# A cross network on one core: product 4 at a second level in both tiles, block 21's residual by DMA, weight loads reordered and held

## The chip, the core and the metric

The kernel runs on one core of a Trainium2 chip. The metric is the device time of one execution in microseconds (us), lower is better. The engines are called by the profile's names: PE is TensorE's matmul row and PEld its weight loads, DVE is VectorE, ACT is ScalarE, POOL is GpSimd, SP is SyncE, which here only issues DMAs.

## The reference

```python
B, F, D, L = 16384, 100, 16, 6
Din = min(F * D, 1024)              # 1024
# x0 [16384, 1024], ws [6, 1024, 1024], bs [6, 1024], all bfloat16
x = x0
for l in range(L):
    proj = jnp.einsum('bd,de->be', x, ws[l]) + bs[l]
    x = x0 * proj + x
return x
```

Six layers; in each, every row of `x` goes through a 1024 x 1024 matrix, gets a bias, is multiplied element by element with the first input, and is added to itself.

## The kernel before

**Tiles and units.** The 16384 rows are cut into 16 tiles of 1024 rows (`pr`, 0 to 15). Two tiles make a group (`grp`); in a group the tile with `lane` 0 and the one with `lane` 1 take turns, layer by layer. One tile in one layer is a unit; there are 96, in the order of `units`. A tile's state `x` lies transposed in one of three SBUF tiles `xst`, its first input in one of three `x0T`. So at any time one `xst` belongs to neither tile of the group: before layer 1 it still holds the output of the group before (its transposes out are issued in layer 0 of the second tile), and from layer 0 of the next group it holds that group's first tile.

**Seven products.** A unit's 1024 x 1024 x 1024 product is done by Strassen's scheme in the Winograd form: seven products of half size, P1 to P7, in place of eight. `T1` to `T4` are input combinations (VectorE), weights 5, 6, 7, 3 are weight combinations, made once in the first group and kept in DRAM (`Lc`). A product at one level is four groups (`m`) of four matmuls of 512 columns (`group`, line 318); its result is evicted from PSUM by ScalarE with the bias (`biased`, line 337). A product at the second level is again cut by seven: `inner` (line 506) issues seven groups of four matmuls of 256 columns, named `5p1` to `5p7` for product 5, and so on. It needs input sums of its own in `ti` tiles (`5t13`, `5t2`, `5t4`; products 2 and 3 share `23t2`, `23t4`), weights of its own (`5i`, `2i`, `3i`, `4i`), seven plain evictions or copies in place of four with bias (`copy`, line 327: two of the seven copy a partial sum from one PSUM bank into another, in which the next group goes on adding), and one more vector add (`5cc`).

Tile 0 and the last unit use one level only (`plain`). All other units have products 5, 2 and 3 at the second level (order list `PE_TWO`). Product 4 is there as well (`PE_FOUR`) where the lane is in `K4[l]`: both tiles in layer 0, the second tile alone in layers 1 to 4, none in layer 5.

**After the products.** The results lie in SBUF blocks `Q`, `U`, `V`, `W` (output blocks 11, 12, 22, 21), `P1s`, `P5s`, `C3`. VectorE adds them up (`Q1`, `Ua`, `Ub`, `Va`, and `Wa` where product 4 is at the second level), multiplies by the first input (`Qm`, `Um`, `Vm`, `Wm`) and adds to the state (`Qx` and so on). Blocks named in `DMA_RES[l]` do without that last vector instruction: GpSimd issues a DMA that adds the block into `xst` (line 563). Before, these are Q, U and V in layers 1 to 4. The names of the seven blocks turn from unit to unit by `NEXT`, so that a block still being read isn't written at once.

**Weights.** `wp` is a ring of 12 slots for 11 weights a layer (10 in layer 5). `ring_seq` is the order of the loads; `pump`, called after every step of the program, issues the next load on SP (line 247) as soon as the program order has passed the last use of the weight 12 places earlier. Both tiles use a loaded weight.

**Order.** Each step is an `Op` with the resources that it reads and writes, an engine and an estimated cost (`occ`, `lat`). `schedule` builds the dependencies, keeps TensorE's steps in the order of the lists at the top (`PE_FIRST` ... `PE_LAST`), and orders the other engines by due times reckoned back from TensorE; `ACCUM` is the latency it assumes for an accumulating DMA. The steps are then issued in that order, which is fixed on every engine. `fence` steps on POOL keep accumulations behind the output's transposes.

Of the kernel before, what the change touches and what calls it, by code (L numbers as in the profile page):

```python
# [9 lines left out]
ADD = mybir.AluOpType.add  # L10
# [12 lines left out]
P3.0 P4.3 P4.1 P4.0 P4.2  # L23
""".split()
PE_TWO = """
5p5 P1.1 5p1 P1.0 P1.3 5p2 2p5 5p6 2p1 P1.2 5p3 2p2 5p7 2p6 P6.0 5p4 2p3 3p5 2p7 3p1 P6.1 2p4 3p2 3p6 P6.2 P6.3 3p3
3p7 P7.0 P7.1 P7.2 3p4 P7.3 P4.1 P4.0 P4.3 P4.2
""".split()
PE_FOUR = """
5p5 P1.0 5p1 2p5 2p1 P1.1 5p2 5p6 2p2 P1.2 2p6 P1.3 5p3 5p7 2p3 2p7 P6.0 3p5 5p4 2p4 P6.1 P6.3 3p1 4p5 P6.2 4p1 3p2  # L30
P7.0 4p2 3p6 4p6 P7.1 3p3 4p3 4p7 P7.2 3p7 4p4 P7.3 3p4
""".split()
PE_LAST = """
P1.0 P1.1 P1.2 P1.3 P2.0 P2.1 P2.2 P2.3 P5.0 P5.1 P5.2 P5.3 P6.0 P6.1 P6.2 P6.3 P3.0 P3.1 P3.2 P3.3 P7.0 P7.1 P7.2 P7.3
# [2 lines left out]
ARRIVE = {"rows0": 4.9, "w0.1": 6.4, "rows1": 8.9, "rows2": 11.3, "w0.2": 11.9, "h0": 14.3, "h1": 15.5, "q": 17.5, "next": 21.0, "raw1": 40.0}  # L37


ACCUM = 9.0  # L40


class Op:
# [81 lines left out]
    return order, start, late  # L125


@with_exitstack
def kernel(
    ctx: ExitStack,  # L130
# [18 lines left out]
    KQ, HQ, NQ = KH // 2, H // 2, NB // 2  # L149
    RING = 12  # L150
    NDUMMY = 8
    K4 = {0: (0, 1), 1: (1,), 2: (1,), 3: (1,), 4: (1,)}
    DMA_RES = {1: "QUV", 2: "QUV", 3: "QUV", 4: "QUV"}

    const = ctx.enter_context(tc.tile_pool(name="const", bufs=1))
    dram = ctx.enter_context(tc.tile_pool(name="dram", bufs=1, space=bass.MemoryType.DRAM))
# [9 lines left out]
    xsts = [work.tile([P, 2, 2, KH, KH, P], BF16, name=f"xst{i}") for i in range(3)]  # L166
# [6 lines left out]
    ip["4"] = ip["2"]  # L173
    P1s, P5s, Q, U, V, W, C3 = (work.tile([P, KH, KH, P], BF16, name=f"ev{i}") for i in range(7))
    EV = {"5c": P5s, "3c": C3, "U": U, "V": V, "W": W, "Q": Q, "P1s": P1s}
    NEXT = {"5c": "3c", "3c": "5c", "U": "W", "V": "U", "W": "V", "Q": "Q", "P1s": "P1s"}
    home = {r: r for r in EV}
    TURNED, rows = ((0, 0), (1, 0), (0, 1)), (P1s, U, V)
    zeros = tin["4"][:, 0]
    ident = const.tile([P, P], BF16, name="ident")  # L180
# [35 lines left out]
    gl_of = lambda u: units[u][0] // 2 * L + units[u][1]  # L216
# [3 lines left out]
    ring_seq = []  # L220
    for gl in range(NGROUP * L):
        if gl < L:
            ring_seq += [(gl, w, "load") for w in RAW] + [(gl, w, "make") for w in MADE]
        else:
            ring_seq += [(gl, w, "load") for w in "1 5 5i 2 2i 6 3 3i 7 4 4i".split()[:11 if gl % L in K4 else 10]]
    slot = {(gl, w): f"slot{i % RING}" for i, (gl, w, _) in enumerate(ring_seq)}
    wt, uses_left, live = {}, {}, []
    pos = {"next": 0}
# [7 lines left out]
        live.append(key)  # L236
        return wt[key]

    def pump():
        while pos["next"] < len(ring_seq):  # L240
            gl, w, kind = ring_seq[pos["next"]]
            if kind == "make":
                return
            t = ring_tile((gl, w))
            if t is None:
                return
            nc.sync.dma_start(t[:], w_src(gl % L, w))
            pos["next"] += 1

    def ring_make(gl, w):  # L250
# [11 lines left out]
    ops, named = [], {}  # L262
# [6 lines left out]
    def op(name, eng, occ, lat, fn, rd=(), wr=(), weights=(), key=None, after=(), due=FAR, at=0.0):  # L269
        rd, wr = [at_home(r) for r in rd], [at_home(r) for r in wr]  # L270
        rd = tuple(rd) + tuple(slot[k] for k in weights if k in slot)
        for k in weights:
            uses_left[k] = uses_left.get(k, 0) + 1
        named[name] = len(ops)
        ops.append(Op(name, eng, occ, lat, fn, rd, tuple(wr), tuple(weights), key, tuple(named[a] for a in after), due, at))

    QD = ((0, 0), (0, 1), (1, 0), (1, 1))
    for u, (pr, l) in enumerate(units):
        one, first, last = plain(u), u == 0, u == NU - 1
        if not first:  # L280
            home = {r: home[NEXT[r]] for r in home}
        P1s, P5s, Q, U, V, W, C3 = (EV[home[r]] for r in ("P1s", "5c", "Q", "U", "V", "W", "3c"))
        CB = {"5": P5s, "2": Q, "3": C3, "4": W}
        gl, grp, lane = gl_of(u), pr // 2, pr % 2
        x0T, xst = x0Ts[pr % 3], xsts[pr % 3]
        xs = x0T if l == 0 else xst
        X0 = {q: f"x0.{pr % 3}.{q[0]}{q[1]}" for q in QD}
# [3 lines left out]
        kmajor = l == 0  # L291
# [15 lines left out]
        def ttop(name, o, a, b, o_, rd, wr, n=KH * NB, **kw):  # L307
            dve(name, lambda: tt(o, a, b, o_), n, rd, wr, **kw)
# [4 lines left out]
        def group(name, w, bank, bname, rhs, rname, m, start, gl=gl, kmajor=kmajor):  # L313
            def fn():
                for k in range(KH):
                    r = rhs[:, k, :] if kmajor else rhs[:, :, k, :]
                    o = bank[:] if kmajor else bank[:].rearrange("p (j r) -> p j r", r=P)
                    nc.tensor.matmul(o, lhsT=wt[(gl, w)][:, k, m * P:(m + 1) * P], rhs=r,  # L318
                                     start=(start and k == 0), stop=(k == KH - 1), skip_group_check=True)
# [30 lines left out]
        def fence(q, sp, u=u):  # L350
            def fn():
                nc.gpsimd.dma_start(seen[:], x0Ts[sp][0:1, q[1], q[0] * KH, 0:32])
            op(f"fence@{u}", "POOL", 0.6, 0.6, fn, [f"x0.{sp}.{q[0]}{q[1]}"], ["xbar"])

        if l == 0 and lane == 1:
            for q in QD:
# [119 lines left out]
        if not one:  # L476
            for X, a, b in (("5", 0, 1), ("2", 2, 3), ("3", 0, 1), ("4", 2, 3))[:len(inn)]:
# [12 lines left out]
                def inner(i, bank, start, X=X, gl=gl, q=q, tk=tk, src=src, kmajor=kmajor):  # L490
                    quad = {1: (0, 0), 2: (1, 0), 3: (1, 1)}
                    rhs = (lambda k: q(*quad[i], k)) if i in quad else (lambda k: tk({4: 3, 5: 0, 6: 2, 7: 1}[i], k))
                    rn = {1: src, 2: src, 3: src, 4: X + "t4", 5: X + "t13", 6: X + "t2", 7: X + "t13"}[i]
                    w = X if i in (1, 2, 4) else X + "i"

                    def fn():
                        if i in (1, 2, 4):
                            k0, e0 = {1: (0, 0), 2: (KQ, 0), 4: (KQ, HQ)}[i]
                            wv = wt[(gl, w)][:, k0:k0 + KQ, e0:e0 + HQ]
                        else:  # L500
                            wi = weight(gl, w) if gl < L else weight(gl, w)[:]
                            wv = wi.rearrange("p q (k e) -> p q k e", k=KQ)[:, {5: 0, 6: 1, 3: 2, 7: 3}[i]]
                        for m in range(KQ):
                            for k in range(KQ):
                                o = pX[bank][:, m * NQ:(m + 1) * NQ]
                                nc.tensor.matmul(o if kmajor else o.rearrange("p (j r) -> p j r", r=P), lhsT=wv[:, k, m * P:(m + 1) * P],  # L506
                                                 rhs=rhs(k), start=(start and m == 0 and k == 0), stop=(k == KQ - 1), skip_group_check=True)
# [38 lines left out]
        allm = lambda s: [f"{s}.{m}" for m in range(KH)]  # L546
        if not last:
            if not one:
                ttop("Q1", Q[:], Q[:], P1s[:], ADD, allm("Q") + allm("P1s"), allm("Q"))
            ttop("Ua", U[:], U[:], P5s[:], ADD, allm("U") + allm("5c"), allm("U"))  # L550
            if not one:
                ttop("Ub", U[:], U[:], C3[:], ADD, allm("U") + allm("3c"), allm("U"))
            if "4" in inn:
                ttop("Wa", W[:], W[:], V[:], ADD, allm("W") + allm("V"), allm("W"))
            ttop("Va", V[:], V[:], P5s[:], ADD, allm("V") + allm("5c"), allm("V"))
            for nm, C, q in (("Q", Q, (0, 0)), ("U", U, (0, 1)), ("V", V, (1, 1)), ("W", W, (1, 0))):
                if l == 0:
# [114 lines left out]
                op(f"sto{q[0]}{q[1]}.{pt}@{u}", "SP", 0.5, 8.0, sto, [sname], ())  # L672

    order, start, _ = schedule(ops)

    ctx.enter_context(tc.manual_schedule(
        engines={nc.tensor.engine, nc.scalar.engine, nc.vector.engine, nc.sync.engine, nc.gpsimd.engine}))
# [28 lines left out]
        load_half("4", h)  # L706
    nc.sync.dma_start_transpose(out=blk(x0Ts[0], 1, 1), in_=x0[NB:2 * NB, H:2 * H])

    held = [i for i in order if ops[i].name.startswith("ld") and ops[i].name.endswith(".1@1")]
    for i in held:  # L710
        ops[i].fn()
    for i in order:
        if i not in held:
# [4 lines left out]
        pump()  # L718


# [28 lines left out]
```

## Time and profile before

| | before |
|---|---|
| median of 3 runs | 2219.56 us (2219.45 to 2220.05) |
| the profiled execution | 2219.68 us, of which its span is 2217.9 us |
| busy: PE, DVE, ACT, POOL | 2208.2, 2144.3, 2037.4, 204.9 us |
| matmuls | 14625 |
| accumulating DMAs (line 563) | 192 of 512 KB |
| weight loads (line 247) | 475 of 512 KB |
| DMA share of two queues | 53.8% (issued by SP), 28.2% (issued by POOL) |
| granted TensorE clock | 0.999 |

The span reaches from the first to the last instruction; 1.8 us of the execution lie around it. Busy time is the union of an engine's instructions; matmuls overlap in the record, so that a matmul of 512 columns is shown with 379 ns although the next one starts 216 ns after it. Instructions of VectorE and ScalarE overlap by some 0.08 to 0.12 us in the same way. The DMA share is the part of the span in which the 16 DMA engines move packets of that queue.

### The profile page before, as it was taken

How to read it: one execution, taken by the hardware profiler on the slowest of the kernel's cores; microseconds unless marked ns; L12 is line 12 of the kernel's file. 1: busy time of each engine (PE TensorE's matmuls, PEld its weight loads, DVE VectorE, ACT ScalarE, POOL GpSimd, SP SyncE). 2: the span in 40 equal slices, each digit the busy share in tenths (PEclk: the TensorE clock that was granted, in tenths of full speed). 3: DMA queues.
4: the chain of work that ended last, by engine and by line, in shares of the span. 5: the costliest groups of instructions: out<-in, count | busy, mean ns of one | idle time of the engine just before them, and what ended most of it. 6: DMA issues, size and time to landing. Idle time of an engine off the chain costs nothing.

```text
span 2217.9 us, 39582 instructions
## 1 busy us (share of the span) xinstructions
PE 2208.2 (100%) x14625; PEld 1427.9 (64%) x14625; DVE 2144.3 (97%) x2527; ACT 2037.4 (92%) x3642; POOL 204.9 (9%) x263
## 2 busy tenths in 40 slices
PE   9999999999999999999999999999999999999998
PEld 5555566666666666666666666666666666666664
DVE  8999999999999999999999999999999999999997
ACT  7888899999999999999999999999999999999997
POOL 1122100110001100011000110011100111001110
PEclk9999999999999999999999999999999999999999
DMA  8777899768996689866898679986799877997777
GB/s 256 207 203 208 201 226 258 190 172 209 259 257 179 173 227 252 256 176 177 228 254 244 171 193 233 265 214 177 207 225 256 217 180 224 224 251 196 200 224 166
DMA packets 454306, 478.66 MB, mean 216 GB/s; under 512 B 269024, under 2 KB 381152, under 8 KB 454112
## 3 DMA queue, kind: packets, MB, share of 16 engines
q1 hardware_dynamic: 418352, 349.49, 53.8%
q0 software_dynamic: 35168, 126.38, 28.2%
q8 instruction: 114, 1.87, 0.3%
q14 instruction: 80, 0.66, 0.1%
q10 hardware_dynamic: 592, 0.27, 0.0%
HBM read 252.72 MB, written 58.20 MB: 140 GB/s over the span
## 4 chain that ended last, share of the span: by engine, by line
PE 98%; DMA 0%; DVE 0%; SPq 0%; issue 0%; POOLq 0%; ACT 0%; DVEq 0%; ACTq 0%
PE pA L318 52%; PE pX L506 43%; PE pX L318 3%; DMA wp<-in_ws_dram 0%; SPq L690 0%; DVE ev L204 0%; DMA xst<-x0T 0%; SPq L697 0%; DVE x0T L204 0%; DVE T L204 0%; POOLq L744 0%; ACT ev L337 0%; DVE x0T L421 0%; SPq L703 0%; SPq L700 0%
## 5 line engine op out<-in xcount | busy, mean ns | idle before, releaser
L506 PEld LDWEIGHTS <-wp 128*128 128x128 bf16 x8424 | 824.2, 98 | 272.3 <-issue 1.0
L337 ACT ACTIVATE ev<-pA,b_all 128x512 bf16<-128x512 f32 x1291 | 883.2, 691 | 114.2 <-PE pA L318 73.7
L318 PE MATMUL pA<-T,wp 128*128 128x512 bf16 x3856 | 924.0, 379 | 0.0
L318 PEld LDWEIGHTS <-wp 128*128 128x128 bf16 x5728 | 560.2, 98 | 493.8 <-issue 2.5
L327 ACT CAST ev<-pX 128x512 bf16<-128x512 f32 x1284 | 700.5, 596 | 22.5 <-PE pX L506 15.0
L506 PE MATMUL pX<-ti,wp 128*128 128x256 bf16 x4748 | 658.0, 273 | 0.0
L204 DVE TENSOR_TENSOR ev<-ev,ev 128x2048 bf16<-128x2048 bf16 x419 | 501.5, 1213 | 44.4 <-ACT ev L327 36.9
L204 DVE TENSOR_TENSOR ev<-ev,x0T 128x2048 bf16<-128x2048 bf16 (+1 forms) x324 | 383.9, 1204 | 1.0
L327 ACT COPY pX<-pX 128x512 f32<-128x512 f32 x628 | 364.6, 593 | 3.6
L318 PE MATMUL pA<-xst,wp 128*128 128x512 bf16 x1280 | 319.5, 379 | 0.0
L563 POOL DMA_DIRECT2D xst<-ev x192 | 166.0, 866 | 1294.6 <-ACT ev L337 491.9
L506 PE MATMUL pX<-xst,wp 128*128 128x256 bf16 x1736 | 260.4, 273 | 0.0
L506 PE MATMUL pX<-T,wp 128*128 128x256 bf16 x1588 | 238.2, 273 | 0.0
L204 DVE TENSOR_TENSOR ev<-ev,ip 128x1024 bf16<-128x1024 bf16 x314 | 209.2, 683 | 0.0
L204 DVE TENSOR_TENSOR T<-xst,T 128x2048 bf16<-128x2048 bf16 x160 | 194.8, 1217 | 2.5 <-PE pX L506 1.6
L204 DVE TENSOR_TENSOR T<-xst 128x2048 bf16<-128x2048 bf16 x160 | 194.8, 1217 | 0.1
L327 ACT CAST ip<-pX 128x512 bf16<-128x512 f32 x314 | 184.8, 589 | 0.4 <-PE pX L506 0.4
L204 DVE TENSOR_TENSOR xst<-ev,xst 128x2048 bf16<-128x2048 bf16 x124 | 150.7, 1217 | 0.0
L204 DVE TENSOR_TENSOR ti<-T,ti 128x512 bf16<-128x512 bf16 x272 | 113.4, 417 | 0.1
L204 DVE TENSOR_TENSOR ti<-xst 128x1024 bf16<-128x1024 bf16 x148 | 101.4, 685 | 8.3 <-PE pX L506 7.8
L204 DVE TENSOR_TENSOR ti<-xst,ti 128x1024 bf16<-128x1024 bf16 x148 | 101.2, 684 | 0.1
L204 DVE TENSOR_TENSOR ti<-T 128x1024 bf16<-128x1024 bf16 x136 | 92.9, 683 | 0.0
(57 smaller groups left out, 698.9 us busy)
## 6 DMA issues: line engine op xcount, KB each, us to landing
wp<-Lc SPq DMA_DIRECT2D x329, 512.0 KB, 6.1
xst<-ev POOLq DMA_DIRECT2D x192, 512.0 KB, 5.1
wp<-in_ws_dram SPq DMA_DIRECT2D x148, 512.0 KB, 6.8
out_dram<-x0T SPq DMA_DIRECT2D x60, 512.0 KB, 4.3
Lc<-wp POOLq DMA_DIRECT2D x24, 512.0 KB, 6.0
Lc<-xst POOLq DMA_DIRECT2D x23, 512.0 KB, 5.3
ev<-in_x_dram SPq DMA_DIRECT2D x3, 512.0 KB, 6.2
wp<-in_ws_dram SPq DMA_DIRECT2D x4, 256.0 KB, 7.5
```

What stands on the lines that cost most here:

```text
L204: nc.vector.tensor_tensor(out=o, in0=a, in1=b, op=op)
L318: nc.tensor.matmul(o, lhsT=wt[(gl, w)][:, k, m * P:(m + 1) * P], rhs=r, start=(start and k == 0), stop=(k == KH - 1), skip_group_check=True)
L327: act(name, lambda: nc.scalar.copy(out=dst, in_=src), rd, wr)
L337: act(name, lambda: nc.scalar.activation(out=dst, in_=src, func=IDENT, bias=b_all[:, c:c + 1], scale=1.0), rd, wr, True)
L506: nc.tensor.matmul(o if kmajor else o.rearrange("p (j r) -> p j r", r=P), lhsT=wv[:, k, m * P:(m + 1) * P], rhs=rhs(k), start=(start and m ...
L563: nc.gpsimd.dma_start(xblk(xst, *q), C[:], accum_op=ADD)
```

## The change

- **Product 4.** `K4` holds both tiles in layers 0 to 4: the first tiles of groups 1 to 7 do product 4 at the second level in layers 1 to 4 too. Layer 5 stays as it was.
- **Block 21.** `DMA_RES` names W as well in layers 1 to 4, so that `Wx` is an accumulating DMA and no vector instruction. `ACCUM` is 9.5.
- **Idle state tile.** In layers 1 to 4 of groups 1 to 7 the second tile's Q, U, V, W lie in the `xst` that belongs to neither tile. `lend` steps stand for the handover in the planner; they issue nothing. `NEXT` is another turn for the blocks that are left.
- **Orders.** `PE_TWO` and `PE_FOUR` hold the same groups in another order; `Ua` is listed after `Ub` and `Wa`.
- **Weight loads.** `LOAD_ORDER` is another order of the same loads. `plan_loads` gives each load from the second group on a planned time: as soon as its slot is free, but moved behind a planned accumulation that it would meet, and no later than `LEAD` + `LOAD` before its first use. `pump(time)` issues a load only when the program order has reached that time, and makes it wait for the newest matmul issued by then.

```diff
 PE_TWO = """
-5p5 P1.1 5p1 P1.0 P1.3 5p2 2p5 5p6 2p1 P1.2 5p3 2p2 5p7 2p6 P6.0 5p4 2p3 3p5 2p7 3p1 P6.1 2p4 3p2 3p6 P6.2 P6.3 3p3
-3p7 P7.0 P7.1 P7.2 3p4 P7.3 P4.1 P4.0 P4.3 P4.2
+5p1 2p5 5p5 P1.1 P1.0 5p6 2p1 5p2 P1.2 P1.3 5p3 2p2 5p7 2p6 P6.0 3p5 5p4 2p7 2p3 P6.1 3p1 P6.2 2p4 3p6 3p2 P7.0 P7.1
+P6.3 3p3 P7.2 3p7 P7.3 P4.0 P4.1 P4.3 3p4 P4.2
 PE_FOUR = """
-5p5 P1.0 5p1 2p5 2p1 P1.1 5p2 5p6 2p2 P1.2 2p6 P1.3 5p3 5p7 2p3 2p7 P6.0 3p5 5p4 2p4 P6.1 P6.3 3p1 4p5 P6.2 4p1 3p2
-P7.0 4p2 3p6 4p6 P7.1 3p3 4p3 4p7 P7.2 3p7 4p4 P7.3 3p4
+P1.1 5p5 5p1 2p5 P1.3 P1.0 5p2 2p1 5p6 P1.2 2p2 2p6 5p3 5p7 P6.0 2p3 3p5 2p7 P6.3 5p4 2p4 P6.2 3p1 P6.1 4p5 3p2 4p1
+3p6 P7.0 4p2 4p6 3p3 P7.1 4p3 3p7 4p7 P7.2 3p4 4p4 P7.3
...
-ACCUM = 9.0
+ACCUM = 9.5
+LOAD, BURST, LEAD = 1.45, 2.9, 8.0
+LOAD_ORDER = "1 5i 2i 5 2 6 3i 3 4i 4 7".split()
...
+def plan_loads(loads, bursts):
+    latest, nxt = [0.0] * len(loads), 1e9
+    for n in range(len(loads) - 1, -1, -1):
+        nxt = min(loads[n][1] - LEAD, nxt) - LOAD
+        latest[n] = nxt
+    busy, t = [], 0.0
+    for b in sorted(bursts):
+        t = max(t, b + 1.0)
+        busy.append((t, t + BURST))
+        t += BURST
+    issue, t = [], 0.0
+    for n, (free, _) in enumerate(loads):
+        s = max(free, t)
+        limit = max(s, latest[n])
+        for a, b in busy:
+            if b > s and a < s + 0.7 * LOAD:
+                s = b
+        t = min(s, limit)
+        issue.append(t)
+        t += LOAD
+    return issue
...
-    K4 = {0: (0, 1), 1: (1,), 2: (1,), 3: (1,), 4: (1,)}
-    DMA_RES = {1: "QUV", 2: "QUV", 3: "QUV", 4: "QUV"}
+    K4 = {l: (0, 1) for l in range(L - 1)}
+    DMA_RES = {l: "QUVW" for l in range(1, L - 1)}
...
-    NEXT = {"5c": "3c", "3c": "5c", "U": "W", "V": "U", "W": "V", "Q": "Q", "P1s": "P1s"}
+    NEXT = {"5c": "3c", "3c": "Q", "U": "U", "V": "W", "W": "V", "Q": "5c", "P1s": "P1s"}
...
-            ring_seq += [(gl, w, "load") for w in "1 5 5i 2 2i 6 3 3i 7 4 4i".split()[:11 if gl % L in K4 else 10]]
+            ring_seq += [(gl, w, "load") for w in LOAD_ORDER if w != "4i" or gl % L in K4]
...
-    def pump():
+    def pump(time=0.0):
         while pos["next"] < len(ring_seq):
             gl, w, kind = ring_seq[pos["next"]]
-            if kind == "make":
+            if kind == "make" or held.get((gl, w), 0.0) > time:
                 return
             t = ring_tile((gl, w))
             if t is None:
                 return
-            nc.sync.dma_start(t[:], w_src(gl % L, w))
+            ld = nc.sync.dma_start(t[:], w_src(gl % L, w))
+            if (gl, w) in held:
+                tc.add_manual_dep(ld.ins, newest["pe"].ins.name, mybir.DependencyInfo(mybir.DependencyClass.Sync, mybir.DependencyReason.DATA))
...
+        idle = (2 * grp + 2) % 3
+        home = dict(cycle)
+        if grp > 0 and lane and 0 < l < L - 1:
+            home.update({r: "S" + r for r in "QUVW"})
+        EV.update({"S" + r: xsts[idle][:, i // 2, i % 2] for i, r in enumerate("QUVW")})
...
+        if grp > 0 and lane == 0 and l in (1, L - 1):
+            op(f"lend@{u}", "POOL", 0.0, 0.0, lambda: None, (), [f"S{r}.{m}" for r in "QUVW" for m in range(KH)] + [f"xs.{idle}.{a}{b}" for a, b in QD])
...
-            ttop("Ua", U[:], U[:], P5s[:], ADD, allm("U") + allm("5c"), allm("U"))
             if not one:
                 ttop("Ub", U[:], U[:], C3[:], ADD, allm("U") + allm("3c"), allm("U"))
             if "4" in inn:
                 ttop("Wa", W[:], W[:], V[:], ADD, allm("W") + allm("V"), allm("W"))
+            ttop("Ua", U[:], U[:], P5s[:], ADD, allm("U") + allm("5c"), allm("U"))
...
+    late_keys = [(n, (gl, w)) for n, (gl, w, _) in enumerate(ring_seq) if gl >= L]
+    plan = plan_loads([(free_at[ring_seq[n - RING][:2]], first_use[k]) for n, k in late_keys],
+                      [start[i] for i, o in enumerate(ops) if o.name[1:3] == "x@" and o.eng == "POOL"])
+    for (_, k), t in zip(late_keys, plan):
+        held[k] = t
```

More of the change, by code (lines that the diff above doesn't have):

```diff
@@ L175 @@
     EV = {"5c": P5s, "3c": C3, "U": U, "V": V, "W": W, "Q": Q, "P1s": P1s}
-    NEXT = {"5c": "3c", "3c": "5c", "U": "W", "V": "U", "W": "V", "Q": "Q", "P1s": "P1s"}
-    home = {r: r for r in EV}
+    NEXT = {"5c": "3c", "3c": "Q", "U": "U", "V": "W", "W": "V", "Q": "5c", "P1s": "P1s"}
+    cycle = {r: r for r in EV}
+    home = cycle
     TURNED, rows = ((0, 0), (1, 0), (0, 1)), (P1s, U, V)
@@ L237, in ring_tile @@
         return wt[key]
-    def pump():
+    held, newest = {}, {}
+    def pump(time=0.0):
         while pos["next"] < len(ring_seq):
             gl, w, kind = ring_seq[pos["next"]]
-            if kind == "make":
+            if kind == "make" or held.get((gl, w), 0.0) > time:
                 return
@@ L280 @@
         if not first:
-            home = {r: home[NEXT[r]] for r in home}
+            cycle = {r: cycle[NEXT[r]] for r in cycle}
+        gl, grp, lane = gl_of(u), pr // 2, pr % 2
+        idle = (2 * grp + 2) % 3
[3 more added lines that the diff above has]
+        EV.update({"S" + r: xsts[idle][:, i // 2, i % 2] for i, r in enumerate("QUVW")})
         P1s, P5s, Q, U, V, W, C3 = (EV[home[r]] for r in ("P1s", "5c", "Q", "U", "V", "W", "3c"))
         CB = {"5": P5s, "2": Q, "3": C3, "4": W}
-        gl, grp, lane = gl_of(u), pr // 2, pr % 2
         x0T, xst = x0Ts[pr % 3], xsts[pr % 3]
@@ L317, in fn @@
                     o = bank[:] if kmajor else bank[:].rearrange("p (j r) -> p j r", r=P)
-                    nc.tensor.matmul(o, lhsT=wt[(gl, w)][:, k, m * P:(m + 1) * P], rhs=r,
-                                     start=(start and k == 0), stop=(k == KH - 1), skip_group_check=True)
+                    newest["pe"] = nc.tensor.matmul(o, lhsT=wt[(gl, w)][:, k, m * P:(m + 1) * P], rhs=r,
+                                                    start=(start and k == 0), stop=(k == KH - 1), skip_group_check=True)
             if first and name in ("P5.0", "P5.1"):
@@ L505, in fn @@
                                 o = pX[bank][:, m * NQ:(m + 1) * NQ]
-                                nc.tensor.matmul(o if kmajor else o.rearrange("p (j r) -> p j r", r=P), lhsT=wv[:, k, m * P:(m + 1) * P],
-                                                 rhs=rhs(k), start=(start and m == 0 and k == 0), stop=(k == KQ - 1), skip_group_check=True)
+                                newest["pe"] = nc.tensor.matmul(
+                                    o if kmajor else o.rearrange("p (j r) -> p j r", r=P), lhsT=wv[:, k, m * P:(m + 1) * P],
+                                    rhs=rhs(k), start=(start and m == 0 and k == 0), stop=(k == KQ - 1), skip_group_check=True)
                     if gl < L and w.endswith("i"):
@@ L674 @@
     order, start, _ = schedule(ops)
+    first_use, free_at = {}, {}
+    for i in order:
+        for k in ops[i].weights:
+            first_use.setdefault(k, start[i])
+            free_at[k] = max(free_at.get(k, 0.0), start[i] + ops[i].occ)
+    late_keys = [(n, (gl, w)) for n, (gl, w, _) in enumerate(ring_seq) if gl >= L]
[3 more added lines that the diff above has]
+        held[k] = t
     ctx.enter_context(tc.manual_schedule(
@@ L707 @@
     nc.sync.dma_start_transpose(out=blk(x0Ts[0], 1, 1), in_=x0[NB:2 * NB, H:2 * H])
-    held = [i for i in order if ops[i].name.startswith("ld") and ops[i].name.endswith(".1@1")]
-    for i in held:
+    early = [i for i in order if ops[i].name.startswith("ld") and ops[i].name.endswith(".1@1")]
+    for i in early:
         ops[i].fn()
     for i in order:
-        if i not in held:
+        if i not in early:
             ops[i].fn()
@@ L717 @@
                 uses_left[k] -= 1
-        pump()
+        pump(start[i])
 _INS = ['x0', 'ws', 'bs']
```

## The prediction

> **What bounds the kernel now.** I read the page first, then the chain that ended last.
>
> ```profile
> PE 2208.2 (100%) x14625; PEld 1427.9 (64%) x14625; DVE 2144.3 (97%) x2527; ACT 2037.4 (92%) x3642; POOL 204.9 (9%) x263
> ...
> PE 98%; DMA 0%; DVE 0%; SPq 0%; issue 0%; POOLq 0%; ACT 0%; DVEq 0%; ACTq 0%
> ```
>
> The chain is TensorE from start to end, but four units stand above 85%, so I asked whether TensorE ever waits. In the table of waits the largest entry of a TensorE matmul past the start-up is this one; the rest of the 2218 us has none.
>
> ```profile
> PE pX L318 <- ACT pX L327: 0.7, 2, 0.5
> ```
>
> So the time is the number of matmuls times their pitch. The chain, piece by piece, gives the pitch: 20 matmuls of 512 columns in 4.32 us, 20 of 256 columns in 2.18 us.
>
> ```profile
> 903.43 4.32 PE pA L318 x20
> ...
> 939.01 2.18 PE pX L506 x20
> ```
>
> That is 0.216 and 0.109 us. A unit (one tile, one layer) with products 5, 2, 3 at the second level has 64 long and 84 short matmuls, 22.98 us; one with product 4 too has 48 and 112, 22.58 us. The x20 pieces recur with that rhythm (538.55 to 561.54 is one unit of the first kind; 903.43 to 949.00, 45.57 us, is one of each).
>
> How near the other engines are, by the table of windows (us, then busy us of PE, PEld, DVE, ACT and POOL, TensorE clock, DMA share, GB/s): one whole group of twelve units, then a pair of units of the middle layers 1 to 4, then the end of layer 5.
>
> ```profile
> 835.11:1108.69 273.58, 273.58 (x1850) 180.81 (x1848) 266.95 (x311) 256.77 (x463) 21.77 (x26) 1.00 0.83 219
> ```
> ```profile
> 949.00:994.57 45.57, 45.57 (x309) 30.14 (x308) 43.86 (x52) 42.77 (x78) 5.15 (x7) 1.00 0.72 197
> ...
> 1085.71:1108.69 22.98, 22.98 (x149) 14.49 (x148) 22.98 (x27) 21.06 (x38) 0.00 (x0) 1.00 1.00 217
> ```
>
> VectorE idles 6.63 us a group, all of it in the middle layers (1.71 us a pair); around layers 5 and 0 it never idles. That is the margin which the change spends.
>
> **The change, part by part.** *Product 4.* It goes to the second level for the first tile of a group too, in layers 1 to 4: 4 layers x 7 tiles (2, 4, ... 14; tile 0 stays at one level) = 28 units. Each loses 16 long matmuls and gains 28 short ones: 16 x 0.216 - 28 x 0.109 = 3.456 - 3.052 = 0.40 us. 28 x 0.40 = **11.2 us off TensorE**, all on the path.
>
> *ScalarE* in such a unit loses 4 biased evictions and gains 7 copies. Their pitch where they run back to back (915.31: four casts in 2.04 us) is 0.48, a biased one 0.58: +1.04 us a unit, +4.2 a group on 256.8 of 272. It costs nothing while TensorE's banks come free in time; a four-product unit already runs beside it at 22.58 us.
>
> *VectorE* gains two instructions of 1024, two of 512 and one of 2048 elements. The pitch, in order of time (start, duration):
>
> ```profile
> 930.17 0.69 DVE L204 TENSOR_TENSOR ev<-ev,ip 128x1024 bf16<-128x1024 bf16 x1
> 930.78 0.69 DVE L204 TENSOR_TENSOR ti<-xst,ti 128x1024 bf16<-128x1024 bf16 x1
> ...
> 931.98 3.49 DVE L204 TENSOR_TENSOR ev<-ev,ev 128x2048 bf16<-128x2048 bf16 x3
> 935.39 3.49 DVE L204 TENSOR_TENSOR ev<-ev,x0T 128x2048 bf16<-128x2048 bf16 x3
> ...
> 944.21 1.23 DVE L204 TENSOR_TENSOR ev<-ev,ev 128x2048 bf16<-128x2048 bf16 x1 [1.26 <-ACT ev L327]
> ```
>
> (935.39 - 931.98)/3 = 1.137 for 2048, 0.61 for 1024, 0.335 for 512: 2 x 0.61 + 2 x 0.335 + 1.137 = 3.02 us a unit. *Block 21's residual* takes one 2048 add (1.137) out of all 64 units of layers 1 to 4. A group: 4 x 3.02 - 8 x 1.137 = **+2.98 us**, 266.95 to 269.9, while TensorE's group shrinks to 273.58 - 1.60 = 271.98. VectorE keeps 2.1 us idle of 6.63. I take it as hidden, for two reasons: the units of layer 0 already have this very mix (product 4, no residual add of their own) and run at about 22.6 us with VectorE never idle; and VectorE is early: the closest result to a matmul that reads it is 3.7 us (an instruction on `ti` ends at 863.95, its matmul starts at 867.65), so it may fall some 3 us back, and a wait like the 1.26 us above vanishes by itself when it runs late. If that cover is gone, the second rival gives the price.
>
> *The added transfers.* 64 accumulations more (192 to 256). In the middle layers of one group:
>
> ```profile
> q0 software_dynamic: 3488, 12.59, 38.4%
> q1 hardware_dynamic: 11167, 23.28, 34.0%
> ```
>
> 24 accumulations hold the 16 engines for 0.384 x 182.28 / 24 = 2.92 us each, 44 weight loads 1.41 each. A pair goes from 6 x 2.92 + 11 x 1.41 = 33.0 to 38.9 of 45.2 us: 72% to 86%. Layers 5 and 0, where the share is 1.00, get none. From issue to landing the accumulations take:
>
> ```profile
> DMA to landing us min/median/max: 4.5/5.1/9.5
> ```
>
> The vector add of block 21 ended at 916.95 for a unit begun near 884.6; its first reader in the next layer, the `2t13` input sum, may now start some 921 to 926. The second-level matmul that needs it, `2p5`, comes 1.3 us or more into a unit begun at 930.2: 5 us or more of cover. On POOL's queue the instruction waits for `Wm`; behind it stand only other accumulations and the fence. Block U is the tight one: its accumulation lands as little as 1.2 us before `T1` reads it, and a third transfer beside it (+2.9) can make VectorE wait 1.7 us; its lag eats that. That `Ua` is now listed behind `Ub` and `Wa` puts U later by up to two adds, 2.3 us, and the new orders ask for `5p5`, which hangs on `T1`, 0.9 us later in a unit: the upper bound is 2.8 us a pair more, if all of it showed. Bounds for all these: 0 to 2.8 us a pair; I take 0, as the 3.7 us above covers one such wait.
>
> *Idle state tile.* Its `lend` steps issue nothing. What it removes, ScalarE waiting for a block still being read, is 0.7 us in the whole run: 0. The new turn of the other buffers changes names only.
>
> *Weight loads.* As many as before. By the order lists the shortest time from a slot's last use to the next weight's first use is 9.5 us before (`3i`: freed by the last matmul of a unit, used 9.5 us into the next) and 13.9 after (`5`). A held load waits on SP for a matmul and is planned at least 8.0 + 1.45 = 9.45 us ahead of its use. Landing:
>
> ```profile
> DMA to landing us min/median/max: 3.1/6.4/11.6
> ```
>
> Median 6.4 leaves 3 us; the 11.6 would be 2 us late. Behind a held load on SP stand other weight loads, the loads of x and the output's transposes and stores; x is loaded over a unit ahead. Bounds: a gain of 0 (no load is waited for now) to 2 us a late load; I take 0, as loads now land as little as 1.1 us before use without loss.
>
> Head (18 us) and tail (the last unit stays at one level) are unchanged. **Sum:** profiled execution 2219.68 - 11.2 = 2208.5; the median, 0.12 lower, 2208.4.
>
> **Two rules against it.** The rows above give 0.216 and 0.109 us a matmul, no faster pace for long ones, and units whose lengths differ by 0.40 us. The Trainium skill, "TensorE: Matmul & The Clock Gate", section Back-to-back issue gap, says that in a stream of weight loads and matmuls both set the spacing: about 131 ns at 512 columns and 81 at 128. By my estimate from that page (98 ns at 256) a changed unit would grow by 28 x 0.098 - 16 x 0.131 = 0.65 us and the kernel by 18 us; the trace disagrees with the figure for 512. Beside the 100% of PE stand 64% of PEld: the skill's "Perfetto Trace Analysis", section Identifying the Most-Contended Engine, says that the share of busy matmul time shows no nearness to the limit, and the share of weight loads does. By that rule TensorE would have slack to lose; here the even pitch and the empty table of waits decide. What both rules would mean is the rival on pitch below.
>
> **Rivals.**
> - *Short stalls of TensorE.* The evictions between second-level products are finished as little as 0.05 us before the next matmul; once a group one matmul comes 0.16 us late. If the new orders cost that in each of 70 units, 11.2 us are gone: 2219.6. At a quarter to a half, 2211 to 2214. Against: the orders still leave a long matmul group or three short ones (1.3 us) between a product and the one that needs its copy.
> - *VectorE becomes the bound* (slower). If its waits for ScalarE stay at 6.63 us a group, a group is 269.9 + 6.6 = 276.5, +2.96 each, 7 groups: +20.7, 2240. It decides where they exceed 273.58 - 269.9 = 3.7 us. For: 99% busy in a fixed order. Against: the lag argument above.
> - *Late weights.* One load a layer 1 us late, 42 layers: 2208 + 42 = 2250; 0.3 us each cancels the gain.
> - *Pitch.* The changed units hold 12 more weight loads of 98 ns each (row of PEld). Were these not beside the matmuls but between them, a unit would grow by 12 x 0.098 - 0.40 = 0.78 us: +21.8, 2241. Against: the second-level units already in the kernel show no such time.
>
> **Chances.** Forecast (2207 to 2210.5) 0.66; short stalls 0.18 (0.13 of it still faster by over 0.2%, the rest the same); VectorE 0.09, of it 0.02 the same; late weights 0.06; pitch 0.01. 0.2% is 4.4 us, about what a measurement of this kernel can tell from no change. Faster 0.79, same 0.07, slower 0.14. The range runs from 2207.0 (the seven stalls of 0.16 us go as well) to 2215.0, which takes in the milder stalls and leaves 0.2 outside.
>
> **What would show it.** Right: the chain's pattern of the middle layers recurs every 45.2 us (a pair of equal units of 22.58), groups last 272.0; VectorE 269 to 271 a group; 256 accumulations, landing 5 to 7 us; DMA share 0.86 in the middle. Wrong: a wait of a matmul on VectorE or a weight load that recurs each layer, units over 22.7 us, landing of weights beyond 9 us.

## The result, and the profile after

The changed kernel takes 2231.41 us (median; 2230.82 to 2233.60) where the kernel before, beside it on the same chip, takes 2220.05: a ratio of 1.0053, 95% interval 1.0042 to 1.0064. It is slower by 0.5%, where 2208.4 us and faster was forecast. Its profiled execution took 2231.83 us, with a span of 2230.1; before, the span was 2217.9. So the spans are 12.2 us apart.

The page first, busy time and the chain that ended last:

```profile
PE 2198.7 (99%) x14913; PEld 1458.9 (65%) x14961; DVE 2163.3 (97%) x2603; ACT 2051.2 (92%) x3726; POOL 256.7 (12%) x327
...
PE 84%; DVE 9%; DMA 4%; issue 1%; SPq 1%; ACT 1%; POOLq 0%; DVEq 0%; ACTq 0%
```

Before, TensorE held 98% of the chain. Now 9% goes through VectorE and 4% through transfers: TensorE waits for something. (48 matmuls are missing from the record; the weight loads show the full 14961, which is 28 units x 12 more than 14625.)

The table of windows, for the same three stretches as before: a group of twelve units, a pair of the middle layers, the end of layer 5 (us, then busy us of PE, PEld, DVE, ACT and POOL, TensorE clock, DMA share, GB/s).

```profile
840.65:1116.03 275.38, 272.52 (x1892) 185.32 (x1896) 271.00 (x323) 259.61 (x475) 28.56 (x34) 1.00 0.90 232
957.02:1002.20 45.18, 44.95 (x319) 30.97 (x318) 44.77 (x55) 43.21 (x81) 6.88 (x8) 1.00 0.85 222
1093.05:1116.03 22.98, 22.98 (x149) 14.40 (x148) 22.63 (x27) 20.84 (x38) 0.53 (x1) 1.00 1.03 207
```

The pair is 45.18 us long, 0.39 less than before, as the sum had it, and layer 5 is unchanged. But the group is 275.38, and not 271.98: 3.4 us are lost somewhere else in it. To find where, I laid the order lists against the matmul rows and took each step's distance to the next one, less its pitch. The first unit of this group lasts 25.55 us (22.74 before); the middle ones 22.59 to 22.62, but for one of 22.99 that waits for a weight. Over the whole span:

| | before | after | difference |
|---|---|---|---|
| matmuls at their pitch | 2196.3 | 2185.3 | -11.0 |
| TensorE beyond its pitch | 3.3 | 21.7 | +18.4 |
| of this: first units of groups 2 to 7 | 1.0 | 11.4 | +10.4 |
| of this: five middle units | 0 | 3.5 | +3.5 |
| of this: unit 12, where group 1 starts | 0 | 1.8 | +1.8 |
| of this: units 2, 4, 6, 8 and 11 of group 0 | 0 | 1.9 | +1.9 |
| from TensorE's last step to the last instruction | 7.1 | 11.4 | +4.3 |
| the rest (head, layout) | | | +0.4 |

The rows marked "of this" leave out some 0.8 us, 0.1 us in many units.

**The first units.** The table of waits names three waits that before had not, or nearly not (there ScalarE waited so for VectorE once, 0.2 us, and for `x0T` nobody waited):

```profile
DVE ti L230 <- DMA x0T<-in_x_dram: 8.5, 6, 2.5
...
ACT ev L372 <- DVE xst L230: 9.1, 13, 1.8
...
PE pX L544 <- ACT pX L362: 7.2, 12, 1.0
```

Six waits of VectorE for the loads of x: one for each of groups 2 to 7. The chain of waits through the first of group 3 shows how the three hang together:

```profile
836.25 7.11 DMA x0T<-in_x_dram
...
843.45 0.06 DVE ti L230
...
863.96 1.24 DVE xst L230
...
865.23 0.02 ACT ev L372
...
865.81 0.60 ACT pX L362
866.41 0.04 issue
866.45 1.47 PE pX L544 x12
```

Block 22 of x for the first tile, which `3t13` reads, lands at 843.36; VectorE has idled 2.5 us for it. VectorE then works without a gap for 20 us, so it stays late; its last addition into the state of the tile that ends here (`xst`, from 863.96) frees a buffer that ScalarE must write next (`E7.0`, line 372; `NEXT` gives V the buffer that W had). ScalarE starts 0.81 us late, the second-level copy behind it on ScalarE (line 362) is late too, and TensorE's group waits for that copy.

The load is late because of its place on SP. The timeline of SP's queue for this group, before and after (start, duration):

```profile
812.60 9.98 SPq L342 DMA_TRANSPOSE x0T<-in_x_dram  x4
...
823.27 3.45 SPq L342 DMA_TRANSPOSE x0T<-in_x_dram  x1
```

```profile
815.63 14.38 SPq L377 DMA_TRANSPOSE x0T<-in_x_dram  x4
830.10 1.01 SPq L275 DMA_DIRECT2D wp<-Lc  x2
831.20 4.38 SPq L377 DMA_TRANSPOSE x0T<-in_x_dram  x1
...
836.25 3.48 SPq L377 DMA_TRANSPOSE x0T<-in_x_dram  x1
```

Eight blocks are loaded, four for each tile. By the order of the steps block 22 of the first tile is the fifth of them before (823.27, 16.0 us ahead of the unit, which begins at 839.27) and the sixth after (836.25, 8.6 us ahead of 844.81); weight loads stand between. The first tile's blocks may be loaded only behind the `let` step (line 382), which waits for accumulations of layer 4's second tile. In the planner's times `let` went from 28.0 to 22.4 us ahead of the unit, and in the trace of group 4 from 30.1 to 24.5, as that tile's V now lands 24.75 us ahead and not 30.4. So the planner lets a second block of the second tile go first. The 14.38 us of the first row hold 3.2 us in which SP stands for it: it overwrites a block that VectorE reads until 822.31, and the first tile's blocks, which `let` had opened at 821.4, stand behind it. And the new order asks for `3t13` 2.6 us earlier in VectorE's plan (4.1 us ahead of the unit, and not 1.6).

**The middle units.** A weight that comes too late, in unit 28 (chain of waits):

```profile
655.26 1.32 PE pX L544 x12
656.58 0.02 issue
656.60 10.89 DMA wp<-in_ws_dram
667.49 0.05 issue
667.54 1.05 PE pX L544 x8
```

The load of weight 2 was issued at 656.60 and landed 10.89 us later, when `2p1` could start. Four middle units lose 2.03, 0.76, 0.40 and 0.11 us so; a fifth loses 0.19 us where VectorE's `T2` comes late. In unit 12 ScalarE's `E6.0` waits 1.81 us for `Ux` of the unit before, the same wait as above.

The rows of the accumulations and weight loads (median us to landing) show which transfers became slower (before: 6.1 and 6.8 for the two rows of weight loads, 5.1 for the accumulations):

```profile
wp<-Lc SPq DMA_DIRECT2D x329, 512.0 KB, 5.6
wp<-in_ws_dram SPq DMA_DIRECT2D x148, 512.0 KB, 6.2
xst<-ev POOLq DMA_DIRECT2D x144, 512.0 KB, 6.6
xst<-xst POOLq DMA_DIRECT2D x112, 512.0 KB, 7.2
```

### The profile page after: what moved, and what is told of

It is laid out like the page before. It is cut to its first block, busy times and chain, and to the rows that moved or that the text cites. A ratio compares the mean times of both kernels' runs of the same rounds, so it can differ in the third digit from the quotient of the medians.

```text
span 2230.1 us, 40486 instructions
## 1 busy us (share of the span) xinstructions
PE 2198.7 (99%) x14913; PEld 1458.9 (65%) x14961; DVE 2163.3 (97%) x2603; ACT 2051.2 (92%) x3726; POOL 256.7 (12%) x327
## 4 chain that ended last, share of the span: by engine, by line
PE 84%; DVE 9%; DMA 4%; issue 1%; SPq 1%; ACT 1%; POOLq 0%; DVEq 0%; ACTq 0%
PE pX L544 42%; PE pA L353 40%; DVE ev L230 4%; DVE xst L230 2%; DVE T L230 2%; PE pX L353 2%; DMA x0T<-in_x_dram 1%; DMA wp<-in_ws_dram 1%; DVE ti L230 1%; DMA xst<-ev 1%; SPq L377 0%; DVE wp L230 0%; ACT ev L372 0%; DMA xst<-x0T 0%; SPq L739 0%
## 5 line engine op out<-in xcount | busy, mean ns | idle before, releaser
L353 PE MATMUL pA<-T,wp 128*128 128x512 bf16 x3377 | 851.3, 379 | 1.6
L372 ACT ACTIVATE ev<-pA,b_all 128x512 bf16<-128x512 f32 x955 | 650.3, 691 | 81.1 <-PE pA L353 48.6
L544 PE MATMUL pX<-ti,wp 128*128 128x256 bf16 x5196 | 721.8, 273 | 2.0 <-ACT ev L362 1.6
L230 DVE TENSOR_TENSOR ev<-ev,ev 128x2048 bf16<-128x2048 bf16 (+1 forms) x307 | 367.6, 1218 | 13.5 <-ACT ev L372 11.8
L544 PE MATMUL pX<-T,wp 128*128 128x256 bf16 x1924 | 288.7, 273 | 6.4 <-ACT pX L362 6.4
L230 DVE TENSOR_TENSOR ev<-ev,x0T 128x2048 bf16<-128x2048 bf16 (+1 forms) x212 | 253.4, 1203 | 1.1
L372 ACT ACTIVATE xst<-pA,b_all 128x512 bf16<-128x512 f32 x224 | 154.6, 690 | 9.5
L602 POOL DMA_DIRECT2D xst<-xst x112 | 96.2, 859 | 523.3 <-ACT ev L362 276.4
L230 DVE TENSOR_TENSOR xst<-xst,x0T 128x2048 bf16<-128x2048 bf16 x112 | 137.0, 1224 | 0.7
L230 DVE TENSOR_TENSOR xst<-xst,ev 128x2048 bf16<-128x2048 bf16 x112 | 136.2, 1222 | 0.3 <-ACT ev L362 0.2
```

The lines of the kernel that those rows point to most:

```text
L230: nc.vector.tensor_tensor(out=o, in0=a, in1=b, op=op)
L353: newest["pe"] = nc.tensor.matmul(o, lhsT=wt[(gl, w)][:, k, m * P:(m + 1) * P], rhs=r, start=(start and k == 0), stop=(k == KH - 1), skip_ ...
L372: act(name, lambda: nc.scalar.activation(out=dst, in_=src, func=IDENT, bias=b_all[:, c:c + 1], scale=1.0), rd, wr, True)
L544: newest["pe"] = nc.tensor.matmul(o if kmajor else o.rearrange("p (j r) -> p j r", r=P), lhsT=wv[:, k, m * P:(m + 1) * P], rhs=rhs(k), sta ...
L602: nc.gpsimd.dma_start(xblk(xst, *q), C[:], accum_op=ADD)
```

## The experiments

The theory: x is loaded late, since the accumulations of layer 4 push `let` back, and with it the first tile's loads on SP. Its rivals: the held weight loads, the fourth accumulation's traffic, or product 4 make the loss by themselves.

**Hold the loads less** (LEAD 14).

```diff
-LOAD, BURST, LEAD = 1.45, 2.9, 8.0
+LOAD, BURST, LEAD = 1.45, 2.9, 14.0
```

> The changed kernel with LEAD = 14.0 for 8.0, so that held loads are issued some 6 us earlier. Theory A, which gives the held loads only the waits of about 3.5 us that occur in five units of the middle layers (the weight 2 landing as its matmul should start): these go, the first units of the groups stay, time about 2228. Rival C (the held loads are the main cost): 2220 or less. If the holding was worth its price, the accumulations land later with the loads in their way, and the time rises above 2232.

Measured: 2253.64 us, ratio 1.0157 [1.0141, 1.0172]. That is the third case of the expectation, 25 us above the first. TensorE's time beyond its pitch is 43.8 us. From its table of waits:

```profile
DVE ti L230 <- DMA xst<-ev: 22.3, 24, 4.8
```

24 waits for accumulations (two after the change, 4.3 us). The weight loads land after 6.6 and 8.9 us in the median (5.6 and 6.2). So to hold the loads until 8 us ahead of their use, and not 14, is worth over 20 us here: to hold them less doesn't win the time back. No run leaves the holding out.

**Only the fourth accumulation** (the kernel before, block 21's residual by DMA, nothing else).

```diff
-    DMA_RES = {1: "QUV", 2: "QUV", 3: "QUV", 4: "QUV"}
+    DMA_RES = {l: "QUVW" for l in range(1, L - 1)}
```

> The kernel before with one part of the change: block 21's residual by DMA in layers 1 to 4 (64 accumulations more), nothing else. Theory A: the accumulations' end, and with it the loads of the first input, come some 1 to 3 us later, but VectorE has 6.6 + 9.1 us of idle time a group now and its waits cost nothing: 2219 to 2221. Rival D (a fourth accumulation a unit is itself too much for the DMA engines, whatever VectorE does): 2224 or more, with waits for accumulations or weights in the middle layers.

Measured: 2232.64, ratio 1.0058 [1.0043, 1.0073]. That is rival D, 12 us above the range of theory A: this part alone loses 13 us, though it takes 9.1 us a group from VectorE. TensorE's time beyond its pitch grows by 9.0 us, most of it in the second tile's unit of layer 1 (units 27, 39, 51, 63, 75, 87: 0.8 to 1.4 us each), the end by 4.0 us. From its table of waits:

```profile
DVE T L204 <- DMA xst<-ev: 18.9, 27, 2.6
DVE ti L204 <- DMA xst<-ev: 11.8, 8, 2.7
```

Here nothing holds the weight loads: they land after 7.7 and 8.0 us in the median. VectorE is busy 59 us less (2085.4 and 2144.3), but now waits 30.7 us for accumulations, and its waits for ScalarE's results grow from 41.6 to 85.0 us.

Nobody waits for x in this run. Five of the six first units lose no more than before, the sixth 0.3 us more, and block 22 is the fifth load again, 16.3 us ahead of unit 36 (which begins at 840.99):

```profile
811.00 10.76 SPq L342 DMA_TRANSPOSE x0T<-in_x_dram  x4
...
824.66 2.85 SPq L342 DMA_TRANSPOSE x0T<-in_x_dram  x1
```

So the fourth accumulation by itself doesn't make x late; what it costs here it costs elsewhere.

**Only product 4** (the kernel before, with product 4 at the second level in both tiles, block 21 by VectorE).

```diff
-    K4 = {0: (0, 1), 1: (1,), 2: (1,), 3: (1,), 4: (1,)}
+    K4 = {l: (0, 1) for l in range(L - 1)}
```

> The kernel before with one part of the change: product 4 at the second level for both tiles in layers 1 to 4, block 21's residual still added by VectorE, old orders and old loads. TensorE's matmuls fall by 11.2 us. VectorE's work in a pair of units of layers 1 to 4 goes from 43.9 to 46.9 us, above TensorE's 45.2. Theory V (VectorE then sets the pace): pairs of about 46.9 us and some 5 us a group more than before, time 2245 to 2260. Rival (it can fall behind in layers 1 to 4 and catch up elsewhere): 2208 to 2215; against that, it never idles in layers 5 and 0 either.

Measured: 2315.04, ratio 1.0433 [1.0417, 1.0448]. Slower, as expected, but by 95 us, and not by 25 to 40. By the sum VectorE's group is 266.95 + 4 x 3.02 = 279 us, 7 us over TensorE's, which makes some 50 us. The page has VectorE busy 2222 of 2318.7 us, so it isn't simply full. Its table of waits:

```profile
DVE T L204 <- DMA xst<-ev: 67.0, 27, 5.6
ACT ev L337 <- DVE xst L204: 52.3, 59, 1.8
...
ACT ev L337 <- DMA xst<-ev: 41.5, 26, 3.7
```

Where VectorE is late, the accumulation is issued late, and VectorE waits for its landing: 67 us. ScalarE waits for the blocks that VectorE or an accumulation still reads: 93.8 us. In the changed kernel, with all parts, these two rows sum to 11.2 us. So product 4 needs other parts of the change; no run adds them one by one, so how much of this the idle state tile removes is not shown.

**Less for the loads of x** (the changed kernel; blocks 21 and 22 of x aren't loaded for the first tiles of groups 2 to 7, so that part of the input is old).

```diff
+                if pt > 2 and pt % 2 == 0 and q[0] == 1:
+                    return
```

> The changed kernel with the loads of the first input's blocks 21 and 22 left out for the first tiles of groups 2 to 7 (12 DMA transposes; those tiles compute with old data there); all orders are the same. Theory A (they land late, VectorE waits for them where it has no slack, ScalarE's evictions then wait for VectorE's reads of the buffers, TensorE for ScalarE): VectorE's six waits for them go, the first units of groups 2 to 7 return from 23.8-25.6 to about 22.8 us, and the time falls by some 10 us to about 2221. Rival B (the new turn of the buffers alone makes ScalarE wait for the former unit's adds): first units stay at 24 us, 2229 to 2231.

Measured: 2222.11, ratio 1.0011 [1.0002, 1.0021]: 9.3 us less than the changed kernel. The first units lose 0.26 us each. This is what the late x costs.

**Only a truer cost for the loads of x** (the planner is told 3.6 us of SP and 8.0 to landing).

```diff
-            op(f"ld{q[0]}{q[1]}.{pt}@{u}", "SP", 2.7, 6.0, fn, ...)
+            op(f"ld{q[0]}{q[1]}.{pt}@{u}", "SP", 3.6, 8.0, fn, ...)
```

> The changed kernel with the planner told that a load of the first input holds SP 3.6 us (2.7) and lands after 8.0 us (6.0), nearer to what was measured; no work is left out, only orders move: VectorE's input sum of product 3 for a group's first unit comes some 5 us later, behind other work. Theory A: VectorE's wait for it goes, the first units of groups 2 to 7 return to some 22.8 us, time 2221 to 2223. Rival B: they stay near 24, time 2229 to 2231. Rival C: unchanged, 2230 to 2232.

Measured: 2228.02, ratio 1.0033 [1.0023, 1.0043]. That lies between the ranges of theory A and rival B: groups 2 and 5 start clean (0.26 us); the other four lose 1.4 to 1.8 us. `3t13` moved 5.5 us back in the plan, but SP let more weight loads in between, so the block came later too.

**The `let` step earlier** (the planner is told that it is due 14 us before).

```diff
+            if ops[i].name.startswith("let"):
+                late[i] -= 14.0
```

> The changed kernel with the small DMA that opens the loads of the first input (let) made more urgent by 14 us for the planner, nothing left out: in the planned order the last accumulation of the second tile's layer 4, and let behind it, come 4.0 us earlier, while VectorE's input sums for the next group stay where they are. Theory A: block 22 lands some 4 us earlier, about 7 us ahead of the unit, VectorE's waits of 1.0 to 2.6 us go, first units of groups 2 to 7 at 22.7 to 23 us, time 2221 to 2224. Rival B: first units stay near 24 us and the time at 2229 to 2231. If the adds that now come later (the first tile's of layer 5) matter more, units of layer 5 grow instead.

Measured: 2221.69, ratio 1.0008 [0.9999, 1.0017], as theory A had it. No VectorE instruction waits for x any more, ScalarE's wait for `xst` falls from 9.1 to 2.0 us, and all six first units lose 0.26. One due time recovers 9.7 us. The timeline of SP's queue for group 3 (unit 36 begins at 842.94):

```profile
813.73 13.08 SPq L379 DMA_TRANSPOSE x0T<-in_x_dram  x4
826.90 0.53 SPq L277 DMA_DIRECT2D wp<-Lc  x1
827.48 3.37 SPq L379 DMA_TRANSPOSE x0T<-in_x_dram  x1
```

The last of these is block 22: the fifth load again, 15.5 us ahead of the unit (16.0 in the kernel before). The `let` step itself lands hardly sooner (23.7 us ahead, and not 23.4); what it changes is the order, in which no second block of the other tile stands ahead any more. So not the traffic makes these 10 us, but the place in the queue. What is left beside the kernel before: 11.2 us beyond the pitch (3.3 before), of it 2.6 in unit 12, and an end of 12.0 us (7.1 before), against 11.0 us saved: together +1.8, measured +2.0.

**Sixty-four tiny transfers** (the kernel before, one DMA of 64 bytes on POOL in each unit of layers 1 to 4). The theory was that the end grows with the number of POOL's DMAs.

```diff
+        if 0 < l < L - 1:
+            op(f"tiny@{u}", "POOL", 0.6, 0.6, lambda: nc.gpsimd.dma_start(seen2[:], ident[0:1, 0:32]), ...)
```

> The kernel before with 64 DMAs of 64 bytes added on POOL's queue, one in each unit of layers 1 to 4, waiting for nothing and waited for by nothing. In the kernels with 64 accumulations more, the end from TensorE's last step to the last instruction took 11.1 to 12.1 us against 7.1, with a DRAIN of POOL that outlasts the last landing by 4 us. Theory N (the closing DRAIN follows the number of DMAs that POOL issued): 11 us at the end here too, time 2223 to 2225. Rival S (it follows the bytes or the accumulations): 7 us, time 2219 to 2221.

Measured: 2221.18, ratio 1.0007 [0.9997, 1.0016]. The end is 7.8 us (7.1): the theory falls.

**Toward a version that beats both.** Three kernels, each on top of the one before it, all with the earlier `let`: the stores of the last first tile get a due time; group 0's block 21 goes back to VectorE; the loads are held 1 us less.

```diff
-                op(f"sto{q[0]}{q[1]}.{pt}@{u}", "SP", 0.5, 8.0, sto, [sname], ())
+                op(f"sto{q[0]}{q[1]}.{pt}@{u}", "SP", 0.5, 8.0, sto, [sname], (), due=NU * 22.7 + 12.0 if pt >= NPAIR - 2 else FAR)
...
-                if nm in DMA_RES.get(l, ""):
+                if nm in DMA_RES.get(l, "") and (grp > 0 or nm != "W"):
...
-LOAD, BURST, LEAD = 1.45, 2.9, 8.0
+LOAD, BURST, LEAD = 1.45, 2.9, 9.0
```

> The changed kernel with the urgent let of the run before (221.7 us over 2000, 2221.7) and a due time for the stores of the last group's first tile, so that the vector adds of its layer 5 and the output's transposes and stores come earlier under the last unit (in the planned order the add of block 22 moves from 12.6 to 3.6 us into it, that of block 21 from 8.1 to 5.8). Theory A (the end lost 4.3 us because three of these stores stood on SP behind the last unit's transposes): the end from TensorE's last step goes from 12 to 7 or 8 us, time 2217 to 2218.5. Rival S (the closing DRAIN of POOL is long wherever there are 64 accumulations more): the end stays at 11 to 12, time 2221 to 2222.

Measured: 2220.34, ratio 1.0001 [0.9993, 1.0010]; 1.4 us less than with `let` alone, the end 10.3 us in the profile (12.0). Less than hoped: the last store now lands 5.4 us after TensorE's last step, as in the kernel before, but the end doesn't return to 7.1 us. This is nearer to rival S.

> As the run before in this list, and block 21's residual in group 0 by VectorE as before the change (8 accumulations fewer, 248). Theory: in group 0 the accumulations share POOL's queue and the DMA engines with the 47 stores of combined weights; VectorE's wait of 5.4 us for an accumulation there and the 2.6 us that the first unit of group 1 loses go: time 2.5 us below the run without it. Rival (the wait comes from the new turn of the buffers in group 0): no difference.

Measured: 2215.85, ratio 0.9984 [0.9975, 0.9993]: 4.5 us less, more than hoped. The 2.1 us of unit 12 and 0.7 of unit 11 are gone; where the rest comes from the traces don't show, as the profiled execution here (2217.55) lies above the median of its kernel and that of the run before (2218.43) was the fastest of its kernel. Two units of it wait 0.9 and 1.2 us for weight 2, as in the changed kernel.

> As the run before in this list, with LEAD = 9.0 for 8.0. Theory A (TensorE still loses 0.3 to 1 us in a few units of the middle layers to weights that land as they are needed): those go, time 0.5 to 1.5 us lower. Rival C (each us of lead puts loads in the accumulations' way: 14.0 cost 22 us): 2 to 4 us higher.

Measured: 2215.66, ratio 0.9980 [0.9971, 0.9989]. By the medians this isn't told apart from the one before. Its profiled execution has no matmul that waits for a weight load, 7.8 us beyond the pitch and an end of 8.8 us. Its page, busy time and chain:

```profile
PE 2199.7 (99%) x14961; PEld 1460.2 (66%) x14961; DVE 2170.5 (98%) x2611; ACT 2054.7 (93%) x3726; POOL 249.7 (11%) x319
...
PE 91%; DVE 5%; issue 1%; DMA 1%; ACT 1%; SPq 0%; POOLq 0%; DVEq 0%; ACTq 0%
```

So the change with two due times, loads held 1 us less and eight accumulations fewer is 0.2% faster than the kernel before and 0.7% faster than as it was made: 2215.66 / 2231.41 = 0.993. Of the 11.0 us that product 4 saves, it keeps about 4.

## Why the prediction was wrong

*TensorE's work: right.* The 11.2 us forecast are 11.0. The changed units last 22.59 us, and the pitch didn't change. The rival on short stalls falls too: the undisturbed changed units are at 22.59 us where the sum had 22.58. So do the rivals on pitch and on VectorE as the bound, for the change as made: VectorE's group is 271.0 us (269.9 forecast) in one of 275.4; in the best version it is 270.6 of 272.28.

*The loads of x, priced at 0: the step that failed.* It stands in "x is loaded over a unit ahead" with its "I take 0", and in "Layers 5 and 0, where the share is 1.00, get none". True, no accumulation is added in those layers. But those of layer 4's second tile end in layer 5's time and release the `let` step; it went 5.6 us back in the plan, and the order of the loads of x with it. The first of these loads runs over a unit ahead, but the block that decides went from 16.0 to 8.6 us ahead and landed 1.5 us ahead. I read when the row begins, and neither its order nor what opens it. The term of 0 measured 9.3 us (the loads left out) to 9.7 us (`let` due earlier). The bounds of 0 to 2.8 us a pair counted only the steps that read an accumulated block.

*What moved `let`.* In group 4 the landing of V's accumulation, which opens it, comes 5.6 us later; 4.6 us of this is the later issue (32.1 us ahead of the unit, and not 36.7), and only 1.0 us the longer way to landing (7.4 us, and not 6.4). In the plan V's multiply stands 33.2 us ahead, and not 38.3. So most of it is the new order of VectorE's work, and not the fuller transfers. The fourth accumulation alone puts `let` 27.7 us ahead of unit 36 (31.4 before, 25.2 in the changed kernel) and leaves the loads in their order. Which of the other parts moves V's multiply no run shows. The planner alone, asked for the changed kernel without the idle state tile, puts `let` 29.5 us ahead; that points to this part, which the prediction also priced at 0, but it is a plan and not a run.

*The cover of 3.7 us: right, and on the wrong edge.* It was the distance from VectorE's result to TensorE's use. When VectorE falls 2.5 us behind, the first to notice is ScalarE, which must write the blocks that VectorE still reads; that distance was not priced, and the table of waits before showed it used up once already (0.2 us). "What it removes, ScalarE waiting for a block still being read, is 0.7 us in the whole run: 0" counted what was there, not what a later VectorE would make of it. And "the new turn of the other buffers changes names only" is too weak: with U kept in one buffer, `E6.0` waits for `Ux` of the very unit before (1.8 us in unit 12).

*Held weight loads: a mild loss, foreseen as a bound.* The plan's "at least 8.0 + 1.45 = 9.45 us ahead" became about 8.1 us ahead in the trace, as the load waits for the newest matmul issued. 11 of 455 loads land less than 1 us ahead of their use, 1 of 455 before (0.8 us; the 1.1 us that I gave was the second). The loss is 3.3 us; the range allowed for more. The run with LEAD 14 shows that to hold them to 8 us earns its place against 14.

*Head and tail unchanged: wrong by 4.3 us, and the cause is in part open.* The last addition into tile 14's state ends 10.3 us into the last unit (5.6 before), so its transposes and stores come later, and the last store lands 9.8 us after TensorE's last step (5.4 before). But that is not the whole: with the due time for the stores the last landing is back at 5.4 us, and the end still takes 10.3 us, 1.7 us less than without it. There POOL's closing drain ends 4.1 us after the last landing, and the same 4.1 us stand in the run with the fourth accumulation alone (10.4 and 6.3 us after TensorE's last step); in the kernel before it is 0.6 us. Both runs have 64 accumulations more; in the run with as many tiny transfers it is 1.5 us, so the number of POOL's DMAs doesn't explain it. What the drain waits for stays open.

*The parts.* I costed each by itself, and three of four at nothing. The runs show that they don't add up: product 4 alone costs 95 us, block 21 by DMA alone 13, all together 11.4. The chance of 0.14 for slower went to VectorE as the bound, late weights and pitch; a load in layer 5 that loses its place because a transfer of layer 4 ends later was no rival of mine.

## What to carry to other kernels

When an edit adds transfers or moves the work that issues them, follow what their landing releases (a buffer handed back, a row of loads that opens) to the transfer that is needed first, and look how the order of that queue changes, even where the edit itself adds nothing. Measure an engine's cover on every edge out of it: the one that writes what it still reads can be shorter than the one that reads its result. And before an edit is given up, look whether a due time in the order is all that is wrong: here one due time recovered 9.7 us.

## What the runs showed of the hardware

- **Accumulations land later where there are more transfers.** At 192 of them the median was 5.1 us to landing, at 256 it is 6.6 to 7.2, with a middle DMA share of 0.85 and not 0.72. The weight load that TensorE waited for longest took 10.9 us, the slowest of all 16.3.
- **SP's queue is held by a transposing load.** From group 2 on a load of x holds it 1.3 to 4.8 us in the changed kernel, a plain 512 KB load mostly 0.3 to 0.55. One place later in the row is therefore worth some 3 us and what stands between. With `let` landing at nearly the same distance (23.7 and 23.4 us ahead) block 22 is issued 15.5 us ahead of the unit as the fifth load and 8.6 as the sixth: 6.9 us in all. I had counted only the landing.
- **The granted clock after a wait.** In the run with product 4 alone the clock was 0.5 for 3.4 us, four times, after TensorE stood still for 2.7 to 4.1 us (start to start): 4 long matmuls took 1.70 us and not 0.86. Three other gaps of 2.7 to 3.1 us were followed by no such stretch. The Trainium skill, "TensorE: Matmul & The Clock Gate", section Part 1: The HAM clock gate, has the half rate follow an idle window of about 3.4 us that runs free of the work. The length agrees; a gap somewhat shorter than the window (2.7 to 2.8 us) was enough three times. In the changed kernel no wait is that long, and the clock stays at 1.0 up to the last matmul.
